# Constant-product filler on TensorE in the idle stretches of a scheduled four-layer bf16 kernel

## The chip, the cores and the metric

The kernel runs on one core of a Trainium2 chip. The metric is the device time of one execution in microseconds (us). A run is called fast or slow by whether it lies within 1.5% of the fastest of its kernel. Two kernels count as "faster" or "slower" only beyond 2%. Engines are named as in the profile: PE is TensorE's matmuls, PEld its weight loads, ACT is ScalarE, DVE is VectorE, POOL is GpSimd, SP is SyncE.

## The reference

Four residual layers over x of 2048 x 512, in bf16: A, B, A, B, each on the layer-normed x, both A layers with the same weights and both B layers too.

```python
# A: attention with a recurrent memory: 64 segments of 32 tokens, 8 memory rows, 32 heads of 128
for s in range(n_seg):
    h = concat([mem, x[segment s]])            # 40 rows
    q, k, v = h @ Wq, h @ Wk, h @ Wv           # each 512 -> 32 x 128
    p = softmax(where(mask, q k^T * scale, -1e9))
    o = (p v) @ Wo
    mem = o[:, :8];  outs.append(o[:, 8:])     # the memory rows feed the next segment
# B: linear attention, 32 heads of 16
qkv = x @ wqkv
pq, pk = phi(q), phi(k)                        # phi(t) = where(t > 0, t + 1, exp(t)) + 1e-6
o = (pq (pk^T v)) / (pq sum(pk) + 1e-6);  return o @ wo

x = x + A(layernorm(x));  x = x + B(layernorm(x))
x = x + A(layernorm(x));  x = x + B(layernorm(x))
```

The weights Wq, Wk, Wv and Wo have 4 MB each and stay on chip for both A layers. The segments form a chain through `mem`; the last rows of an A layer must be done before the B layer's sum over all tokens is, and so each change of layer is a short serial chain.

## The kernel before

The program is first recorded as nodes (engine, cost, what is read and written), then a list scheduler lays the nodes out on a modelled clock, and that fixes each engine's queue. The chip runs each queue in its order; a node's position is decided by the model's times and by hand-tuned priorities (`OFFSET`), never at run time.

```python
MODE_SLACK = 12.41
LOOK = 0.074

def c_pe4(n_mm, n):                      # model: n_mm products on four column strips, us
    return n_mm / 4.0 * max(0.0255, (n / 2.4 + 3.0) * 1e-3)

    def schedule(self):
        ...
        for nd in nodes:
            nd.prio = nd.tail
            if nd.key is not None and OFFSET:
                step, name, k = nd.key
                nd.prio = -(step * PERIOD + OFFSET[name][k])
        ...
            # in pick_for(e): do not start low-priority PE work if better work is due within LOOK us
            if pick is not None and e == "pe" and any(
                    t <= tn + LOOK and nd.done is None and nd.prio > pick.prio + 1.0 for t, _, nd in pend[e]):
                heapq.heappush(ready[e], (-pick.prio, pick.idx, pick))
                return None
            return pick
```

The loads: Wq, Wk and Wv on ACT's queue, Wo in four parts and then the B weights wqkv (1.5 MB) on SP's queue. The same SP queue also issues the DMA transposes of `turned`.

```python
    P.at(-8000, "ld1")
    add("sp", lambda s: s.dma_start(x_sb[:, 0, :], x_view[0]), 0.4, writes=[("x", 0)], dsem="dx0", lat=2.0)
    ...
        late.append(add("act", lambda a, W=W, v=v: a.dma_start(W[:, :, :], v), 0.5, writes=[nm], dsem="d" + nm, lat=t))
    ...
    for i in range(4):
        ...
        add("sp", lambda s, hs=hs: s.dma_start(Wo_sb[:, hs, :], wo_view[:, hs, :]), 0.9, writes=[("Wo", i)],
                 dsem="dWo%d" % i, after=[late[1 + i // 2]], lat=(12.5, 14.5, 7.3, 9.8)[i])
    add("sp", lambda s: s.dma_start(wqkv_sb[:, :, :], B_wqkv.rearrange("(c p) f -> p c f", p=128)), 0.5,
        writes=["wqkv"], dsem="dwqkv", after=[P.nodes[-1]], lat=5.0)
```

Most products run in a mode of four column strips of 32: one group is four matmuls and four weight loads, eight PE instructions.

```python
        def project(W, key, blk, bkeys, b, urgent):
            ...
                        r = pe.matmul(tl.f32()[32 * j:32 * j + 32, 0:512], blk[:, c, :], W[:, c, o:o + 512],
                                      start=(c == 0), stop=(c == 3), tile_position=(0, 32 * j))
        ...
        for s in range(NSEG):            # the loop over segments of an A layer
            ...
        w = out_block(NSEG)              # last output product, residual, then the B layer's input rows
        residual(NT - 1, 3, w)
        b_in(base + NSEG + 2, NT - 1, not first)
```

The softmax here doesn't subtract the row's maximum and nothing guards it: scores larger than these inputs give would overflow.

## Time and profile before

| kernel before | value |
|---|---|
| time, median of 3 runs | 1845.87 us (1845.44 to 1850.28) |
| span of the profiled run | 1843.1 us |
| PE busy, matmuls / weight loads | 1758.4 us (95%), 46693 / 46693 |
| packets of the instruction queue | 365, 5.98 MB |
| first Wk / Wv / Wo product starts | 25.61 / 39.55 / 51.11 us |
| last residual of layer 1, first Wq product of layer 3 | 900.11, 918.99 us |
| last residual of the second A layer | 1806.27 us |

Here "layer 1" and "layer 3" are the two A layers. PE is the bound except in three places: the first 70 us, where weights load; the 19 us between the layers; and the last 37 us. A page slice is a fortieth of the span; the digits are tenths.

### The profile page before, as it was taken

The page shows a single profiled execution, that of the slowest core. Times are in us where ns is not written, and L with a number is a line of the kernel's source. Part 1 is how long each engine was busy: PE and PEld are TensorE (multiplying, and loading weights), DVE is VectorE, ACT ScalarE, POOL GpSimd, SP SyncE. Part 2 cuts the span into 40 slices and gives each one's busy share as a digit, 9 for nine tenths or more (in the row PEclk, how much of TensorE's full clock was granted, in tenths as well). Part 3 has the DMA queues.
Part 4 walks back from the last instruction along what each step waited for, and adds up shares of the span by engine and source line. Part 5 has one row for each costly group of instructions (what it writes and reads, how often), then busy time and mean ns, then how long its engine had stood idle before and what let it go on. Part 6 is the DMA issues. An engine that isn't in the chain of part 4 may idle for free.

```text
span 1843.1 us, 100858 instructions
## 1 busy us (share of the span) xinstructions
PE 1758.4 (95%) x46693; PEld 1194.1 (65%) x46693; DVE 1017.6 (55%) x3168; ACT 1207.6 (66%) x3127; POOL 76.9 (4%) x182
## 2 busy tenths in 40 slices
PE   5899999999999999999799999999999999999997
PEld 2566676666666767666566666666666666666663
DVE  2355555555555555555545555566555556555566
ACT  3566666766666666666466667666667666666665
POOL 3000000000000000000000000000000000000000
PEclk8999999999999999999899999999999999999999
DMA  9312122212221221211012122122122222122223
GB/s 366 85 37 42 38 44 35 47 38 44 38 41 41 35 46 38 44 37 38 22 29 39 37 41 46 39 42 43 38 41 46 41 43 41 41 43 41 52 62 99
DMA packets 218934, 94.85 MB, mean 51 GB/s; under 512 B 202536, under 2 KB 212656, under 8 KB 216976
## 3 DMA queue, kind: packets, MB, share of 16 engines
q1 hardware_dynamic: 211312, 60.22, 17.7%
q0 software_dynamic: 5616, 15.60, 2.9%
q10 hardware_dynamic: 1584, 12.58, 1.7%
q8 instruction: 365, 5.98, 1.3%
q14 instruction: 57, 0.47, 0.1%
HBM read 29.63 MB, written 10.49 MB: 22 GB/s over the span
## 4 chain that ended last, share of the span: by engine, by line
PE 83%; DMA 11%; ACT 3%; DVE 2%; issue 1%; ACTq 0%; DVEq 0%
PE pb L777 38%; PE pb L987 16%; DMA arena_sb<-arena_sb 9%; PE pb L959 3%; PE pb L861 3%; PE pb L1029 3%; PE pb L799 3%; PE pb L1137 3%; PE pb L916 2%; ACT arena_sb L608 2%; PE pb L878 2%; PE pb L1173 1%; DMA Wk_sb<-in_A_Wk_dram 1%; PE pb L892 1%; PE pb L891 1%
## 5 line engine op out<-in xcount | busy, mean ns | idle before, releaser
L608 ACT ACTIVATE arena_sb<-pb 128x512 bf16<-128x512 f32 (+6 forms) x1412 | 727.2, 523 | 359.8 <-PE pb L777 302.1
L777 PE MATMUL pb<-Wq_sb,arena_sb 128*32 128x512 bf16 x5120 | 357.5, 383 | 0.6 <-DMA Wq_sb<-in_A_Wq_dram 0.6
L777 PE MATMUL pb<-Wv_sb,arena_sb 128*32 128x512 bf16 x5120 | 356.9, 382 | 0.1
L777 PE MATMUL pb<-Wk_sb,arena_sb 128*32 128x512 bf16 x5120 | 343.5, 381 | 6.6 <-DMA Wk_sb<-in_A_Wk_dram 5.2
L987 PE MATMUL pb<-Wo_sb,arena_sb 128*32 128x256 bf16 x10368 | 326.4, 273 | 5.8 <-issue 3.7
L987 PEld LDWEIGHTS pb<-Wo_sb,arena_sb 128*32 128x32 bf16 x10368 | 261.5, 96 | 34.8 <-DVE arena_sb L895 13.8
L944 DVE TENSOR_TENSOR arena_sb<-arena_sb 32x256 bf16<-32x256 bf16 x512 | 213.3, 417 | 119.8 <-ACT arena_sb L940 108.7
L609 DVE CAST arena_sb<-pb 128x128 bf16<-128x128 f32 (+3 forms) x334 | 118.5, 355 | 252.5 <-PE pb L1012 201.4
L609 DVE COPY arena_sb<-pb 128x512 bf16<-128x512 bf16 (+2 forms) x352 | 137.7, 392 | 204.5 <-PE pb L799 198.9
L777 PEld LDWEIGHTS pb<-Wk_sb,arena_sb 128*32 128x32 bf16 x5120 | 141.8, 97 | 126.1 <-DMA Wk_sb<-in_A_Wk_dram 5.3
L777 PEld LDWEIGHTS pb<-Wq_sb,arena_sb 128*32 128x32 bf16 x5120 | 133.4, 97 | 113.6 <-DVE arena_sb L609 24.2
L777 PEld LDWEIGHTS pb<-Wv_sb,arena_sb 128*32 128x32 bf16 x5120 | 134.4, 98 | 86.3 <-issue 4.4
L608 ACT ACTIVATE outW_sb<-pb 128x128 fp32r<-128x128 f32 x261 | 72.3, 277 | 114.4 <-PE pb L987 77.1
L799 PEld LDWEIGHTS pb<-id_sb,arena_sb 128*32 128x32 bf16 x4352 | 77.5, 97 | 90.8 <-ACT arena_sb L608 58.1
L959 PE MATMUL pb<-arena_sb 128*128 128x128 bf16 x1024 | 130.9, 217 | 0.0
L799 PE MATMUL pb<-id_sb,arena_sb 128*32 128x128 bf16 x4352 | 109.6, 221 | 14.7 <-ACT arena_sb L608 14.6
L946 DVE TENSOR_TENSOR arena_sb<-arena_sb 32x64 bf16<-32x64 bf16 x512 | 111.1, 217 | 15.8
L960 PE MATMUL pb<-arena_sb 128*128 128x32 bf16 x1024 | 118.3, 177 | 0.0
L868 ACT ACTIVATE arena_sb<-pb 128x256 bf16<-128x256 f32 x252 | 96.1, 383 | 27.3 <-PE pb L861 20.6
L861 PE MATMUL pb<-arena_sb 128*128 128x32 bf16 x2016 | 97.0, 178 | 5.2 <-DMA arena_sb<-arena_sb 4.9
L895 DVE TENSOR_TENSOR arena_sb<-pb,arena_sb 128x128 bf16<-128x128 f32 x252 | 72.2, 286 | 42.0 <-ACT arena_sb L883 27.6
L861 PEld LDWEIGHTS pb<-arena_sb 128*128 128x128 bf16 x2016 | 74.6, 96 | 30.0 <-DMA arena_sb<-arena_sb 6.4
(121 smaller groups left out, 2304.5 us busy)
## 6 DMA issues: line engine op xcount, KB each, us to landing
arena_sb<-arena_sb SPq DMA_TRANSPOSE x368, 2.5
Wq_sb<-in_A_Wq_dram ACTq DMA_DIRECT2D x1, 4096.0 KB, 13.6
Wk_sb<-in_A_Wk_dram ACTq DMA_DIRECT2D x1, 4096.0 KB, 24.3
Wv_sb<-in_A_Wv_dram ACTq DMA_DIRECT2D x1, 4096.0 KB, 34.6
Wo_sb<-in_A_Wo_dram SPq DMA_DIRECT2D x4, 1024.0 KB, 11.6
xs_scratch<-x_sb POOLq DMA_DIRECT2D x32, 128.0 KB, 2.1
pq_scratch<-arena_sb POOLq DMA_DIRECT2D x32, 128.0 KB, 2.8
x_sb<-xs_scratch POOLq DMA_DIRECT2D x16, 128.0 KB, 2.3
```

Of the source, the lines that this page charges most:

```text
L608: return e.activation(o() if callable(o) else o, i() if callable(i) else i, ACTF.Copy)
L609: return e.tensor_copy(o() if callable(o) else o, i() if callable(i) else i)
L777: r = pe.matmul(tl.f32()[32 * j:32 * j + 32, 0:512], blk[:, c, :], W[:, c, o:o + 512], start=(c == 0), stop=(c == 3), tile_position=(0, 32 ...
L799: r = pe.transpose(tt.bf16()[32 * j:32 * j + 32, 128 * i:128 * i + 128], img[:, k, o:o + 32], id_sb[:, :], tile_position=(0, 32 * j))
L861: r = pe.matmul(tl.f32()[:, o:o + 32], kk[:, hh, :, :].rearrange("p j x -> p (j x)"), qT[:, r2, hh, :, 0:8], start=True, stop=True)
L868: add("act", lambda a: a.activation(Pm[:, k, :, :].rearrange("p a q -> p (a q)"), tl.f32()[:, 0:256], ACTF.Exp, scale=SCALE), c_act(256), ...
L895: add("dve", lambda v: v.tensor_tensor(oTb[:, s % NO, 16 * b:16 * b + 16, 0:8], pv.f32()[:, 0:128].rearrange("p (n q) -> p n q", q=8), Rm[ ...
L944: add("dve", lambda v, q=q, j=j: v.tensor_tensor(Pbx[q, :, j, 0:32], Px[q, :, :], Rx[q, :, :], ALU.mult), c_dve(256) + 0.075, reads=["Px", ...
L946: add("dve", lambda v, q=q, j=j: v.tensor_tensor(Pbx[q, :, j, 32:40], PLL[q, g2, :, gl], Rx[q, :, 0:8], ALU.mult), c_dve(64) + 0.075, read ...
L959: pe.matmul(o, vimg[:, r2, e], Pbx[:, hh, :, 0:32], start=True, stop=False)
L960: return pe.matmul(o[:, :, 0:8], vleft[:, g2, e], Pbx[:, hh, :, 32:40], start=False, stop=True)
L987: r = pe.matmul(tl.f32()[32 * j:32 * j + 32, 0:256], oT[:, 4 * hh + n, :], Wo_sb[:, 8 * n + hh, 256 * d:256 * d + 256], start=(hh == 0 and ...
```

## The change

The intent: PE works at half clock for a while after it idled, so let it run products of two constants (the identity and a tile of ones, into a bank of its own) at the lowest priority wherever it would idle. Then it should be at full clock when the real work comes. All priority offsets were tuned anew with the filler in, and two loads' modelled latency was made more realistic.

```diff
-MODE_SLACK = 12.41
+MODE_SLACK = 12.48
 OFFSET = {
     ... (every offset changed)
+    "warm": (2000.00,),
 }
-    def x_move(o, i, k, reads, writes, kind, eng="pool"):
+    def x_move(o, i, k, reads, writes, kind, eng="pool", lat=2.0):
 ...
-    add("sp", lambda s: s.dma_start(x_sb[:, 0, :], x_view[0]), 0.4, writes=[("x", 0)], dsem="dx0", lat=2.0)
+    add("sp", lambda s: s.dma_start(x_sb[:, 0, :], x_view[0]), 0.4, writes=[("x", 0)], dsem="dx0", lat=8.5)
 ...  (lat=8.5 likewise for the second tile of x in the A layers)
+    def warm(step, n, after):
+
+        P.at(step, "warm")
+        tl = P.tile()
+
+        def mm(pe):
+            for j in range(4):
+                r = pe.matmul(tl.f32()[32 * j:32 * j + 32, 0:128], id_sb[:, 0:32], one_sb[:, :], start=True, stop=True,
+                              tile_position=(0, 32 * j))
+            return r
+        for i in range(n):
+            if i:
+                P.again()
+            add("pe", mm, c_pe4(4, 128), reads=["id", "one"], tiles=[tl], mode="col", after=after if i == 0 else ())
 ...
         prepare(0, -2)
+        if first:
+            warm(base, 210, [n for n in P.nodes if n.key == (base - 2, "prepF", 5)])
 ...
         w = out_block(NSEG)
+        warm(base + NSEG, 230 if first else 170, [P.nodes[-3]])
```

## The prediction

> **What bounds the kernel now.** I read the page first. Its engine table gives TensorE (PE) 95% of a span of 1843.1 us, against 66% for ACT and 55% for DVE, and the chain that ended last is 83% PE. Then I looked for the places where this is not so: the page's 40 slices.
>
> ```profile
> PE   5899999999999999999799999999999999999997
> PEclk8999999999999999999899999999999999999999
> DMA  9312122212221221211012122122122222122223
> ```
>
> PE is full except in the first slice, around slice 20 and at the end, and in the same slices the granted clock (second row) dips. DMA is saturated in the first slice only. Next I asked for the stretches around these places, 5 us each; columns are the window, its length, PE, weight load, DVE, ACT, POOL busy time, granted clock, DMA share, GB/s.
>
> ```profile
> 20.00:25.00 5.00, 0.41 (x16) 0.23 (x16) 0.42 (x1) 0.00 (x1) 2.94 (x9) 0.97 1.01 416
> 25.00:30.00 5.00, 4.38 (x56) 1.97 (x60) 0.30 (x1) 1.19 (x2) 0.00 (x0) 0.50 1.01 418
> ...
> 40.00:45.00 5.00, 5.00 (x51) 1.74 (x44) 2.94 (x10) 1.87 (x5) 0.00 (x0) 0.50 1.03 259
> ...
> 900.00:905.00 5.00, 1.63 (x8) 0.89 (x9) 2.40 (x5) 0.55 (x3) 1.08 (x2) 0.70 0.07 26
> 905.00:910.00 5.00, 4.58 (x32) 2.09 (x30) 2.20 (x7) 1.19 (x2) 0.00 (x0) 0.62 0.10 26
> ```
>
> PE idles, then works at half clock just when it is needed. Cutting windows until the clock was constant gives six cold stretches, each close to 6.83 us long: 24.9 to 31.7, 38.5 to 45.3 and 62.4 to 69.2 while the kernel starts, 902.1 to 908.9 and 915.7 to 922.6 between the layers, 1806.6 to 1813.4 before the last stage. PE is busy in them for 6.07, 6.22, 6.18, 4.61, 4.54 and 3.54 us, 31.2 us together. At half clock up to half of that, **15.6 us or 0.8% of the span, is all that warmth alone can return**. The Wq products at 14.4 us also run cold (629 ns mean, as against 380 in steady state), though the record shows full clock there, as it begins only at 18.0 us; they end long before Wk lands and cost nothing.
>
> **What the Trainium skill says.** "TensorE: Matmul & The Clock Gate", section "Part 1: The HAM clock gate (the "warmup" mystery)", says the array starts at half clock, is released after about a 3.4 us window of activity and throttled again after an idle one, with windows that run free. The trace agrees: the states are 0.50 and 1.00, and cold stretches last two such windows (6.83 us). Under "HAM oscillation — how this bites in real kernels" it asks for no idle gaps above some 3.4 us; here the trace differs: an idle time of 2.5 us (59.9 to 62.4) was followed by a cold stretch, and so was 35.1 to 38.5, where PE was merely half idle. "Part 4: PE-mode transpose" says that transposes don't count as busy for the clock; the filler is a true product, so this favours it. "Runtime: NRT & Kernel Launch", section "Instruction fetch mechanics", says instructions are fetched in blocks of 256 through DMA and that this is mostly hidden. The trace has 365 packets of the instruction queue for 100858 instructions (5.98 MB), so it agrees on the size, but PE shows "issue" waits of 1.2 us at 36.96 and 1.9 us at 1802.5, just when or after DMA is saturated.
>
> **The change part by part.** It adds 210 + 230 + 170 = 610 groups of four products of 128x128 on the four column strips: 2440 matmuls and as many weight loads, 5.2% more than 46693. It takes one group as 56 ns; the transposes of line 799 have the same shape and take 0.22 us for 16 on the chain, so 55 ns for four: agreed, when warm. Added as work this would be 610 x 0.056 = 34 us (1.9%). But the groups have the lowest priority and are placed by the kernel's own scheduler in gaps, and not if better work is due within 0.074 us. PE idles about 12 us before Wv is in, some 10 us between 899.5 and 919 (9.55 of 19.5 us busy) and 4.4 us of the 9.4 from 1805.6 to 1815, so the budgets of 11.8, 12.9 and 9.5 us fit these gaps. I count the filler itself as free, apart from a small delay per real product behind it.
>
> *Start.* Wq lands near 14.3 us, Wk at 25.6, Wv at 1.8 + 34.6 = 36.4; that is bandwidth (416 GB/s at DMA share 1.0), which the filler cannot touch. But Wv's products start at 39.55 only, 3.1 us late:
>
> ```profile
> 25.61 3.60 PE pb L777 x32
> ...
> 36.96 1.23 issue
> ...
> 39.74 5.12 PE pb L777 x47
> ```
>
> This is the chain of waits by time: start, us, what. Warm, the stretch from 25.6 saves some 3.0 us (half of 6.07), so that the backlog is gone when Wv lands; the 48 Wv products (12 rounds of four, 0.43 us each cold, 0.22 warm) save 2.6 us. So 5.7 us of PE time. The next gate is Wo: its last quarters are issued at 38.6 and take 7.8 and about 10 us, landing near 49, and the output product starts at 50.9. That leaves 1.7 us, plus 1.4 to 2.2 us if the issue follows Wv's landing at once (it stands behind a DMA transpose issued at 37.2). I take **3.5 us**, the smaller bound. At 56.0 a DMA transpose takes 6.2 us behind the wqkv load and PE idles 3.05 us, then runs cold; the 210 groups are mostly used by then. If a few are left there, half of 6.18 is saved; I give that one chance in three: **1.0 us**.
>
> *Between the layers.* The chain of waits from 900 to 920:
>
> ```profile
> 903.35 0.62 PE pb L750 x4
> ...
> 904.48 3.61 PE pb L1137 x8
> 908.11 0.61 ACT arena_sb L608
> 908.76 0.41 PE pb L1149 x4
> ...
> 918.01 0.61 PE pb L750 x4
> 918.62 0.43 PE pb L1245 x4
> 919.05 3.75 PE pb L777 x36
> ```
>
> Warm, the eight rows take 1.75 us, but phi(k), which runs beside the second four (1.9 us on ACT and DVE), then ends last, so 1.6 saved; two transposes 0.2 each; lines 1149 and 1245 together 0.2; the 36 products from 919.05 save 1.8. Sum 4.0. Nine PE operations of the chain may find filler in flight or in the wrong place; at one group of 0.056 each plus a change of tiling mode, I take off 0.7 (an estimate from the group's time): **3.3 us**.
>
> *Before the end.* Line 1137 runs four rows on the chain in 1.90 us, warm 0.95; the transpose and the product before it save 0.3; less 0.25 for the filler: **1.0 us**. After that ACT and DVE set the pace, and PE was warm already.
>
> *The new order.* Every priority offset is tuned anew, and the first loads' modelled latency goes from 2.0 to 8.5 us, which is what the profile shows. Steady state has some 2% idle PE, about 35 us over the run; a new order can move that either way. I put 0 +- 5 us.
>
> Sum: 3.5 + 1.0 + 3.3 + 1.0 = 8.8 us, so **1837.0 us**.
>
> **The rivals.** (1) *DMA keeps the start*: the gain of 4.5 shrinks to 1 or 2, because Wo and the wqkv load gate the first steps. DMA share near 1 until 45 us speaks for it; the late Wv products against. Time: 1840. (2) *Filler in the way*: the queue is fixed in order, so filler placed by a model that errs stands before real work, and cold groups take double. The gaps are mostly waits for DMA, though, and the chains' modelled times match (0.60 us for a 512 ACT, 0.70 DVE). If each of the three places loses 2 us: 1843. (3) *Instruction fetch*: 1680 extra instructions while DMA is saturated, about 6.6 blocks; one or two more waits of 1.2 us. For it: the wait at 36.96; against: waits in idle time are free. Time: 1839. (4) *The order decides*: the new offsets cut steady idle by 5 to 8 us: 1830.
>
> **Range and chances.** Start 1.5 to 7, middle 2 to 4.5, end 0.3 to 1.5, order +-5; combined, a gain of 2 to 16 us: 1830 to 1844. For 2% the time must be under 1809 or over 1883; the cold total of 15.6 us and the filler's whole 34 us both stay within that, so "same" is nearly certain.
>
> **What would show it.** Right: no cold stretch left at 25 to 45, at 900 to 922 and at 1807 to 1813, mean clock above 0.995; Wv's products starting at 36.5 and the eight rows near 1.8 us; PE busy share up by about 1%, with no gain from that. The end of the first layer's last output product (899.5 before) shows the start plus the order; from there to about 923 shows the middle. Wrong: filler beside new PE waits, cold stretches at the same places (then constants don't count as activity), "issue" waits that grow, or a shift that grows steadily from 70 to 895 us, which would be the order and not the warmth.

## The result, and the profile after

| | before | after |
|---|---|---|
| median of all 4 runs, us (range) | 1846.95 (1845.44 to 1850.28) | 1873.41 (1871.39 to 1882.19) |
| span of the profiled run | 1843.1 | 1872.7 |
| PE matmuls recorded / weight loads | 46693 / 46693 | 49019 / 49133 |
| packets of the instruction queue | 365 | 384 |
| first Wk / Wv / Wo product | 25.61 / 39.55 / 51.11 | 45.03 / 58.98 / 72.4 |

The kernel takes 1.5% longer: ratio 1.015, 95% interval 1.0114 to 1.0186. That is within 2%, as predicted, but the time lies far above the range of 1830 to 1844, and it is a loss and not a gain. Ratios here are the mean time of one kernel's fast runs over that of the other's of the same rounds, so not quite the ratio of the medians in the table. The weight loads rose by exactly the 2440 of the filler; some matmul records are missing.

By the marks of the two traces the 29.6 us of the spans divide as follows. From the start to the first Wo product: +21.3. From there to the first layer's last residual: 849.0 before, 849.5 after, so +0.5. From that residual to the first Wq product of layer 3: 18.9 before, 24.6 after, +5.7. From there to the second A layer's last residual: 887.3 and 887.4, +0.1. From there to the end: 36.8 and 38.8, +2.0. **The long steady stretches, 94% of the time, did not change by more than one kernel's own scatter (some 4 us a layer, see e9); the loss lies in the three places that were to gain.**

The page's slices of the kernel after, the same three rows as the prediction shows:

```profile
PE   4899999999999999999999999999999999999998
PEclk8899999999999999999999999999999999999999
DMA  8411221221212221212011222222222122222222
```

The dip of PE and clock in the middle is gone from the page (of two cold stretches of 6.8 us one of 3.4 is left, 928.3 to 931.7), so the filler does count as work for the clock. But the start is no warmer, and DMA, which was at 9 and 3 tenths in the first two slices, is at 8 and 4: the same loads are spread out further. The stretches of 5 us, with the columns of the prediction's table:

```profile
25.00:30.00 5.00, 2.92 (x112) 2.92 (x116) 0.00 (x0) 0.00 (x0) 0.00 (x0) 0.71 1.01 416
...
40.00:45.00 5.00, 3.56 (x140) 3.39 (x144) 0.00 (x0) 0.00 (x0) 0.00 (x0) 0.66 0.07 22
```

From 25 to 30 us ACT and DVE do nothing at all, though Wk is there from 25.7; from 40 to 45 us even DMA is nearly idle (share 0.07, before 1.03). What PE does is in its timeline (start, us, engine, line, operation, out<-in, shape, count, and in brackets the idle time ahead and what ended it):

```profile
27.08 3.60 PE L737 MATMUL pb<-one_sb,id_sb 128*32 128x128 bf16 x128 [4.44 <-issue]
34.38 3.38 PE L737 MATMUL pb<-one_sb,id_sb 128*32 128x128 bf16 x128 [3.70 <-issue]
41.12 3.41 PE L737 MATMUL pb<-one_sb,id_sb 128*32 128x128 bf16 x128 [3.37 <-issue]
...
45.03 1.94 PE L793 MATMUL pb<-Wk_sb,arena_sb 128*32 128x512 bf16 x32
```

Line 737 is the filler. It runs in lots of exactly 128 matmuls, which with their 128 loads are 256 instructions, and before each lot PE waits 3.4 to 4.4 us for nothing that the profile shows. The Trainium skill, "Runtime: NRT & Kernel Launch", section "Instruction fetch mechanics", says that instructions come in blocks of 256 over a DMA queue. The lots agree with that number, and so do the packets of queue q8, if they are PE's alone: 365 for 93386 PE instructions before, 384 for 98266 after (twice the weight loads). (The prediction set them against the 100858 of all engines.) In the DMA records of this trace single packets of that queue lie at 24.6, 31.8 and 38.6 us, each about 1.1 us long, and PE goes on about 1.4 us after each ends. The last two start 4.7 and 4.2 us after the first product of the lot before, as if a block were asked for only then. So PE seems starved of instructions: one block per 7.30 us (27.08 to 34.38) and per 6.74 us (34.38 to 41.12). Only after three such blocks come the Wk products, 19.4 us later than before, though Wk landed as early (24.6 us after its issue, before 24.3).

Later work follows. SP's queue in the trace of after:

```profile
53.18 2.11 SPq L806 DMA_TRANSPOSE arena_sb<-arena_sb  x1
55.34 1.19 SPq L647 DMA_DIRECT2D Wo_sb<-in_A_Wo_dram  x2
```

and of before:

```profile
37.23 1.30 SPq L790 DMA_TRANSPOSE arena_sb<-arena_sb  x1
38.59 1.62 SPq L646 DMA_DIRECT2D Wo_sb<-in_A_Wo_dram  x2
```

The second half of Wo stands behind a transpose whose input comes from PE by way of ACT. That transpose is 16 us late, so the load is 16.8 us late, and DMA stands nearly idle between 40 and 55 us (mean share 0.08, before 0.71).

Between the layers the same shows with DMA nearly idle. The chain of waits of after:

```profile
923.60 1.97 PE pb L737 x128
925.57 2.05 issue
927.63 0.35 PE pb L737 x11
```

Again a lot of 128, warm this time (1.97 us), and a wait of 2.05 us: 256 instructions in 4.03 us (923.60 to 927.63), at a DMA share of 0.11. The packet comes 1.4 us after the lot's first product here. And filler is now the chain itself.

### The profile page after: what moved, and what is told of

Same layout as the page of the kernel before. It is cut to its first block, busy times and chain, and to the rows that moved or that the text cites. A ratio compares the mean times of both kernels' runs of the same rounds, so it can differ in the third digit from the quotient of the medians.

```text
span 1872.7 us, 105613 instructions
## 1 busy us (share of the span) xinstructions
PE 1778.8 (95%) x49019; PEld 1232.5 (66%) x49133; DVE 1019.3 (54%) x3175; ACT 1203.5 (64%) x3120; POOL 76.8 (4%) x182
## 4 chain that ended last, share of the span: by engine, by line
PE 81%; DMA 11%; DVE 4%; issue 3%; ACT 2%; POOL 0%; POOLq 0%; ACTq 0%; DVEq 0%
PE pb L793 37%; PE pb L1003 16%; DMA arena_sb<-arena_sb 10%; PE pb L815 3%; PE pb L1045 3%; PE pb L877 3%; PE pb L975 3%; PE pb L737 2%; DVE arena_sb L610 2%; PE pb L1156 2%; PE pb L894 2%; PE pb L932 2%; ACT arena_sb L609 2%; PE pb L1192 1%; PE pb L1274 1%
## 5 line engine op out<-in xcount | busy, mean ns | idle before, releaser
L609 ACT ACTIVATE arena_sb<-pb 128x512 bf16<-128x512 f32 (+5 forms) x1411 | 722.8, 520 | 358.7 <-PE pb L793 294.0
L793 PE MATMUL pb<-Wq_sb,arena_sb 128*32 128x512 bf16 x5120 | 348.9, 380 | 6.0 <-DVE arena_sb L610 5.0
L1003 PE MATMUL pb<-Wo_sb,arena_sb 128*32 128x256 bf16 x10368 | 321.0, 273 | 4.6 <-issue 2.3
L610 DVE CAST arena_sb<-pb 128x32 bf16<-128x32 f32 (+3 forms) x351 | 127.1, 363 | 258.6 <-PE pb L1028 204.2
L610 DVE COPY arena_sb<-pb 128x512 bf16<-128x512 bf16 (+1 forms) x336 | 134.8, 402 | 228.5 <-PE pb L815 218.7
L815 PE MATMUL pb<-id_sb,arena_sb 128*32 128x128 bf16 x4352 | 108.5, 220 | 17.1 <-ACT arena_sb L609 17.1
L877 PEld LDWEIGHTS pb<-arena_sb 128*128 128x128 bf16 x2016 | 74.6, 96 | 31.6 <-DMA arena_sb<-arena_sb 9.3
L975 PEld LDWEIGHTS pb<-arena_sb 128*128 128x128 bf16 x1024 | 89.8, 96 | 5.7 <-issue 1.2
## 6 DMA issues: line engine op xcount, KB each, us to landing
Wk_sb<-in_A_Wk_dram ACTq DMA_DIRECT2D x1, 4096.0 KB, 24.6
```

The lines of the kernel that those rows point to most:

```text
L609: return e.activation(o() if callable(o) else o, i() if callable(i) else i, ACTF.Copy)
L610: return e.tensor_copy(o() if callable(o) else o, i() if callable(i) else i)
L815: r = pe.transpose(tt.bf16()[32 * j:32 * j + 32, 128 * i:128 * i + 128], img[:, k, o:o + 32], id_sb[:, :], tile_position=(0, 32 * j))
L877: r = pe.matmul(tl.f32()[:, o:o + 32], kk[:, hh, :, :].rearrange("p j x -> p (j x)"), qT[:, r2, hh, :, 0:8], start=True, stop=True)
L975: pe.matmul(o, vimg[:, r2, e], Pbx[:, hh, :, 0:32], start=True, stop=False)
L1003: r = pe.matmul(tl.f32()[32 * j:32 * j + 32, 0:256], oT[:, 4 * hh + n, :], Wo_sb[:, 8 * n + hh, 256 * d:256 * d + 256], start=(hh == 0 and ...
```

## The experiments

There are eighteen, each compared with runs of the kernel before on the same chip. "New order" below means the offsets and latencies of the changed kernel.

### e1 to e4: what of the change costs the time

**e1: the new order without filler.**

```diff
-        if first:
-            warm(base, 210, ...)
-        warm(base + NSEG, 230 if first else 170, [P.nodes[-3]])
```

> The new order and the new latency of the first loads, with both calls of the filler taken out. Theory F (instruction supply: the filler's 8 instructions per 56 ns outrun the fetch, and real products stand behind it in PE's queue): the order costs nothing, since layer 2 took 885.2 us after as against 886.6 before; 1840 to 1852 us, and Wk's products start near 25.6 us. Rival O (the new order costs the time): stays above 1862. Rival T (the filler's PE time stands in the way): also near 1846, so this run separates O from F and T only.

Measured: median 1845.91, ratio 1.0002 (0.9979 to 1.0025). Wk, Wv and Wo start at 25.73, 38.41 and 49.64. The new order and latencies cost nothing and gain nothing in the sum; by its trace the first A layer is 3.4 us longer and the second 5.3 us shorter than before.

**e2: the same queue, the same filler time on PE, a quarter of its instructions.** One full-width product takes the place of four strips; the scheduler is told nothing, so all places stay.

```diff
-            for j in range(4):
-                r = pe.matmul(tl.f32()[32 * j:32 * j + 32, 0:128], id_sb[:, 0:32], one_sb[:, :], ..., tile_position=(0, 32 * j))
-            return r
+            return pe.matmul(tl.f32()[:, 0:128], id_sb[:, :], one_sb[:, :], start=True, stop=True)
```

> Each filler group is one full 128x128x128 product in place of four 32-column ones: by the scheduler's costs the same order, place and 56 ns of PE time, but 2 instructions in place of 8 (1220 in place of 4880). Theory F: at 36 instructions per us it stays under the 64 per us that the trace of the changed kernel shows between the layers (one block of 256 per 4.0 us), so the issue waits in the filler go from 22 us to under 4 and the time to 1835 to 1846. Rival T (PE time of filler in the way): nothing changes, 1868 to 1878.

Measured: 1850.52, ratio 1.0032 (1.0012 to 1.0051). PE's timeline:

```profile
21.32 6.76 PE L736 MATMUL pb<-one_sb,id_sb 128*128 128x128 bf16 x118
28.01 1.91 PE L790 MATMUL pb<-Wk_sb,arena_sb 128*32 128x512 bf16 x32
```

118 groups run in 6.76 us without a gap, 57 ns each, and Wk's products start at 28.01, not at 45.03. The page shows a clock of 9 in all slices, though cold stretches remain (38.3 to 41.7, 65.6 to 69.0 and 1809.8 to 1816.7 us, at 0.50). Some 23 of the 28 us are gone with the instructions, in each of the three places: from the start to Wo 51.7 us (after 72.4, before 51.1), between the layers 17.1 (24.6, 18.9), at the end 34.7 (38.8, 36.8). The time still missed the expected 1835 to 1846, because the two A layers took 855.6 and 892.7 us (before 849.0 and 887.3); e14 to e18 look for the cause.

**e3: the same instructions, almost no work.** The filler has 8 columns, not 128.

```diff
-                r = pe.matmul(tl.f32()[32 * j:32 * j + 32, 0:128], id_sb[:, 0:32], one_sb[:, :], ...)
+                r = pe.matmul(tl.f32()[32 * j:32 * j + 32, 0:8], id_sb[:, 0:32], one_sb[:, 0:8], ...)
```

> All 8 instructions of each group are kept, and the order, but the products have 8 columns in place of 128, so PE's array works far less. Theory F: the same instruction count means the same waits for instructions, 1866 to 1882 us (a little more cold clock), Wk's products again start near 45 us. Rival T: with the array time gone the loss goes too, 1842 to 1852.

Measured: 1874.80, ratio 1.0163 (1.0142 to 1.0184): the whole loss, with a sixteenth of the filler's columns.

```profile
26.08 1.19 PE L737 MATMUL pb<-one_sb,id_sb 128*32 128x8 bf16 x128 [5.03 <-issue]
32.83 1.19 PE L737 MATMUL pb<-one_sb,id_sb 128*32 128x8 bf16 x128 [5.55 <-issue]
```

A lot of 128 now takes 1.19 us (in after 3.4 to 3.6), and the wait grows to 5.0 and 5.6 us, so that the period stays at 6.75 us. **The period belongs to the instructions, not to the work in them.** e2 and e3 together settle the main cause: the supply of instructions to PE.

**e4: the fewest instructions.** One product of 512 columns in the place of four groups, with the right cost and mode given to the scheduler.

```diff
+            return pe.matmul(tl.f32()[:, :], id_sb[:, :], one_sb[:, :].unsqueeze(1).to_broadcast([128, 4, 128]), start=True, stop=True)
-        for i in range(n):
+        for i in range(n // 4):
-            add("pe", mm, c_pe4(4, 128), ..., mode="col", ...)
+            add("pe", mm, c_pe(1, 512), ...)
```

> The same budget of PE time in 152 products of 128x512 (304 instructions in place of 4880). Theory F: no issue wait is left in the filler, no cold stretch before 60 us, between the layers or before the end; 1832 to 1842 us, which is what the blind prediction expected of the change itself. Rival T: coarser pieces of 0.22 us stand in the way even more, 1870 or above.

Measured: 1847.99, ratio 1.0016 (0.9997 to 1.0035), mean clock 0.998, above the expected 1832 to 1842. The loss is gone, yet a clock that is full but for 37.2 to 40.7 and 64.6 to 68.0 us gained nothing either. Two lines of its timeline show where the start's gain went:

```profile
21.38 6.43 PE L736 MATMUL pb<-one_sb,id_sb 128*128 128x512 bf16 x29
...
62.25 0.37 PE L874 MATMUL pb<-arena_sb 128*128 128x32 bf16 x8 [2.35 <-DMA arena_sb<-arena_sb]
```

The filler ends at 27.8, 2 us after Wk has landed (25.7), and Wk's first product starts at 27.74, because the model puts more of it there than fits: real work stands behind it. And at 62 us PE waits for a DMA transpose. The same line in e1:

```profile
62.77 0.37 PE L877 MATMUL pb<-arena_sb 128*128 128x32 bf16 x8 [4.21 <-DMA arena_sb<-arena_sb]
```

With or without filler PE goes on at 62.2 to 62.8: what is gained before is waited for there.

At the end the rows run warm (1.67 us), and still the last stage takes 36.9 us (before 36.8), where the small products of e2, of about the same PE time in all, take 34.7: in e4's chain of waits wide filler products of 0.22 us each stand between the real ones, which may be why. So wide is not free either.

### e5 and e6: which place costs how much

**e5: filler in the start only** (the call with 230 and 170 groups removed).

> The changed kernel with its first filler alone (210 groups while the weights load). By the trace of the changed kernel the start costs 21.8 us (the last output product of layer 1 feeds its residual at 921.9 us as against 900.1), so 1863 to 1871 us, with Wk's products again near 45 us and the second half of Wo issued near 55 us. If the loss belonged to the filler as a whole and not to places, it would be a third of it: near 1855.

Measured: 1864.96, ratio 1.0111 (1.0094 to 1.0128), so +20 us. **e6: filler between the layers only** (the other calls removed).

> The changed kernel with its second filler alone (230 groups between the layers). By the trace the stretch from the residual of layer 1 to the first Wq product of layer 2 is 24.6 us as against 18.9, so +5.7: 1848 to 1854 us. Theory F says that the DMA is idle here, so one block of 256 instructions still takes about 4.0 us and the filler outruns it without any weight load beside it. If saturated DMA were needed for the loss, this run would be at 1842 to 1846.

Measured: 1853.93, ratio 1.0055 (1.0039 to 1.0072), +9 to +10 us, of which the trace shows 2.9 in the stretch between the layers (21.8 against 18.9) and the rest later. No load runs there (DMA share 0.02 from 918.25 to 921.73), so a loss does not need a busy DMA. The two add up to the whole loss within the scatter.

### e7 to e9: does the start gain if the transfer at 56 us is moved

**e7: no filler, and the wqkv load cut in four.** Its quarters go out in steps 1 to 4.

```diff
-    add("sp", lambda s: s.dma_start(wqkv_sb[:, :, :], ...), 0.5, writes=["wqkv"], dsem="dwqkv", ..., lat=5.0)
+            if first and 1 <= s <= 4:
+                add("sp", lambda e, c=s - 1: e.dma_start(wqkv_sb[:, c, :], B_wqkv[128 * c:128 * c + 128, :]), 0.5, ..., lat=3.0)
```

> No filler; the load of the 1.5 MB wqkv, which stands ahead of the DMA transposes of step 1 in the same queue, is cut in four and issued after steps 0 to 3. Theory D (in the start the transposes behind that load are the gate: PE idled 4.2 us until 62.8 in the run without filler, and all variants resume at 62.2 to 63): the idle time shrinks to under 1.5 us, 1839 to 1844. Rival: each quarter delays a later transpose by as much, and the time stays at 1846.

Measured: 1840.31, ratio 0.9979 (0.9963 to 0.9995). The first residual product comes at 68.17 and not at 71.08 as in e1 (69.52 in e6, whose start is the same). **e8: the same with e4's wide filler.**

> The wide filler (one 128x512 product for four groups) with the same cut load. Theory D says that the wide filler gained nothing at the start because the transposes came at 62 us whatever PE did before; with the gate gone it should be 2 to 5 us under the kernel without filler and the same cut. Rival P (wide filler is itself placed ahead of Wv's products, which started at 41.9 us as against 38.4 without it): no gain, or 1 to 3 us slower than the kernel without filler.

Measured: 1847.3, ratio 1.0014 (0.9999 to 1.0029). Its first residual product comes at 68.58: no gain over e7, although PE's clock is full from 28 to 61.7 us (then 0.50 until 68.5). The filler again lost what it gave. The whole is 7 us slower than e7, more than either expectation allowed; both A layers are longer (852.1 and 888.7 us, in e7 848.3 and 882.7).

**e9: e7 once more, to see its scatter.**

> The same kernel as e7, once more beside the next three, as the level to compare them with: 1838 to 1844 us.

Measured: 1842.13, ratio 0.997 (0.9934 to 1.0005). A third time, as e16 below, it gave 1844.24. The means of 1840.8, 1842.3 and 1843.9 are one kernel's, so **a difference under some 3 us between two kernels of one run each says nothing here.**

### e10 to e15: filler that costs few instructions, place by place

All of these have e9 as their base (new order, wqkv in four), and the filler as one full product per group.

**e11: filler in the middle (198 groups) and at the end (128).**

> e7 with the quarter-instruction filler (one 128x128x128 product per group) between the layers and before the end only, its number cut to 198 and 128 so that none is left over for the steady state. From the segments of e2: 1.8 us saved between the layers (17.1 as against 18.9) and 2.1 at the end (34.7 as against 36.8): 1835 to 1839 us. If instruction places (theory A) matter more than the gain: 1840 to 1846.

Measured: 1846.25, ratio 0.9996 (0.9966 to 1.0026), a miss of the expected 1835 to 1839. The two places did gain (17.2 and 35.2 us, in e9 18.4 and 37.0), but the second A layer took 892.3 us (884.7).

**e12: a start filler trimmed to 132 groups, as wide products.**

> e7 with the wide filler at the start only, cut to the 33 products that stand ahead of Wk's first product (none behind it). Theory P (in e8 filler stood ahead of Wv's products and made them start at 40.3 us): here Wk starts near 25.8 us and runs warm, Wv's products start at 36.5 to 38.5, and layer 1 ends 1 to 3 us earlier: 1836 to 1841 us. If the start is bound by the loads and transposes anyway, the time equals e7's.

Measured: 1844.13, ratio 0.9984 (0.9953 to 1.0015). Wv's products start at 37.91 (e9: 39.02) and the first residual product at 67.2 (e9: 68.83). Eight traces with the same start and no filler there have 68.17 to 68.89, so the start can gain 1.0 to 1.7 us, if little filler stands before Wk (26.28); in the time of the whole it can't be seen.

**e13: filler before the end only (128).**

```diff
+        if not first:
+            warm(base + NSEG, 128, [P.nodes[-3]])
```

> e7 with the cheap filler before the end only (128 groups of one product). By the segments of e11 the end takes 35.1 us as against 37.0 and nothing before it can change: 1.5 to 2.5 us under e16, about 1839 to 1841. If it isn't under e16, the gain at the end is scatter.

Measured: 1840.95, ratio 0.997 (0.9953 to 0.9986), the best kernel with that of e7. The line of the first rows of its last stage in the chain of waits (start, us, what):

```profile
1808.85 1.67 PE pb L1157 x7
```

and in e16, which has no filler:

```profile
1811.68 3.04 PE pb L1158 x7
```

Of the eight products seven are recorded in each; they take 1.67 us warm and 3.04 cold. The stage takes 35.2 us against 36.7 (e16), 37.0 (e9) and 36.8 (before). The mean times of e13 and e16, from the same rounds, differ by 4.1 us; what the end does not explain of that is not explained.

**e14: filler between the layers only (198).** The edit is e13's with `if first` and 198.

> e7 with the cheap filler between the layers only (198 groups of one product). Segment theory: 1.5 us under e16. Theory L (a filler there makes layer 2 slower, as e11's trace has it): 2 to 6 us over e16.

Measured: 1847.35, ratio 1.0015 (0.9998 to 1.0031). **e15: the same queue with 8 columns in each filler product**, so that it keeps no clock.

```diff
-            return pe.matmul(tl.f32()[:, 0:128], id_sb[:, :], one_sb[:, :], start=True, stop=True)
+            return pe.matmul(tl.f32()[:, 0:8], id_sb[:, :], one_sb[:, 0:8], start=True, stop=True)
```

> e14 with 8 columns per filler product: same instructions, order and PSUM banks, no warmth. Theory L by places or banks: as far over e16 as e14 plus the lost 1.5 us. If e14's loss came with the warm clock itself: equal to e16 within 1.5 us. If e14 has no loss: 0 to 2 us over e16.

Measured: 1850.87, ratio 1.0029 (1.001 to 1.0049). The first Wq products of layer 3 in the chain of waits, e14:

```profile
916.40 2.06 PE pb L787 x36
```

and e15:

```profile
919.83 3.96 PE pb L787 x36
```

The same 36 products at half clock take 3.96 us, and warm 2.06. From the last residual to the end of these products it is 19.2 us in e14, 23.3 in e15 and 22.7 before. The mean times differ by 3.2 us (1850.8 and 1847.6), with runs of e15 that scatter over 9 us. So warmth between the layers is worth some 3 to 4 us, close to the 3.3 predicted. But e14 as a whole is not faster than its base: the second A layer takes 890.6 us in it and 890.9 in e15 (from the first Wq product to the last residual), and 884.7 and 887.1 in e9 and e16. No filler product is left over in that layer, and the real products stand in e9's order. So something that comes with the filler and not with warmth seems to take back the 3 us or more (e7, the same kernel as e9 and e16, has 882.7: its own scatter is 4.4 us).

**e10: 104 more PE instructions (52 small products) at the very start, no filler.** Before e11 to e15 the suspicion was that a shift of every later instruction against the blocks of 256 matters.

> e7 with 52 tiny products (104 instructions) put into one early PE step, where PE idles; order, banks and filler as in e7, only every later PE instruction lies 104 places further on in the 256-instruction blocks, as it does in e8 in layer 1. Theory A (the steady state depends on where the fetches of instruction blocks fall): over 3 us away from e7, toward e8's 1847. If the time stays within 2 us of e7, block positions do not explain why e8 was 7 us slower.

Measured: 1844.31, ratio 0.9985 (0.9952 to 1.0019): no effect to be seen.

### e16 to e18: what slows the layer after the filler

**e16: the base again, as a level on the same chip.**

> The kernel without filler and with the cut wqkv load once more, as the level for e13 to e15: 1838 to 1844 us, and again 3 to 6 us under the kernel before.

Measured: 1844.24, ratio 0.9992 (0.9976 to 1.0007). **e17: the base with its PSUM banks renamed**, as a filler tile renames them.

```diff
-    P = _Prog(nc, banks)
+    P = _Prog(nc, [banks[i] for i in (7, 2, 1, 5, 4, 0, 6, 3)])
```

> e16 with the eight PSUM banks renamed everywhere as e14's filler renames them in layer 2; not one instruction more. If the banks' numbers are what costs e14 and e15 their 7 us in layer 2: 5 to 14 us over e16 (both layers have it), 1847 to 1858. If not: 1839 to 1846.

Measured: 1844.45, ratio 0.9995 (0.9978 to 1.0012): the banks are not it. **e18: 140 more instructions at the start**, the same shift modulo 256 as e14 has in the second A layer.

> e16 with 70 tiny products (140 instructions) in an early PE step: all later PE instructions stand in the fetched blocks where e14's stand in layer 2 (396 more, 140 modulo 256). If the places are what costs: 5 to 14 us over e16. If not: 1839 to 1846, and the cause of layer 2's loss stays open.

Measured: 1847.57 (1841.68 to 1852.47), ratio 1.001 (0.9988 to 1.0031), with 890.6 us for the second A layer in the profiled run, as in e14. But the runs scatter over 11 us, so this neither shows nor excludes the shift. Its trace shows something else, too: the start has no "issue" wait near 37 us (1.2 to 1.7 us in the other traces without filler there), no cold stretch from 31.8 us to the end of the layer, and the first residual product at 64.82, over 3 us earlier than in the eight traces named at e12. So where the blocks end may be worth more at the start than filler is; it is one trace, and no run repeats it.

| kernel | median, us | ratio to before (95%) | second A layer in its trace, us |
|---|---|---|---|
| after | 1873.41 | 1.015 (1.0114 to 1.0186) | 887.4 |
| e3, same instructions, no work | 1874.80 | 1.0163 (1.0142 to 1.0184) | 885.8 |
| e2, quarter of the instructions | 1850.52 | 1.0032 (1.0012 to 1.0051) | 892.7 |
| e4, wide filler | 1847.99 | 1.0016 (0.9997 to 1.0035) | 889.1 |
| e1, no filler | 1845.91 | 1.0002 (0.9979 to 1.0025) | 882.0 |
| e14, middle | 1847.35 | 1.0015 (0.9998 to 1.0031) | 890.6 |
| e16, none, wqkv in four | 1844.24 | 0.9992 (0.9976 to 1.0007) | 887.1 |
| e13, end, wqkv in four | 1840.95 | 0.997 (0.9953 to 0.9986) | 886.8 |

## Why the prediction was wrong

**"I count the filler itself as free": this step failed.** Its cost was looked up as PE time (0.056 us per group; a warm lot of after has 32 groups in 1.97 us, 62 ns each) and as gaps in PE's schedule. It was not set against the supply of instructions. A group is eight instructions in 0.056 us, 143 per us; PE got 256 per 6.7 to 7.3 us (35 to 38 per us) while the loads ran, and 256 per 4.03 us (64 per us) at the middle. By the records 640 filler products stand ahead of Wk's first product in the in-order queue, 532 of them, 133 groups, behind the first Wq product: 1064 instructions, 4.2 blocks. The scheduler took these for 7.5 us. They stretch from 19.53 to 45.03 us, 25.5 us; part of that fell where PE had idled before too, and Wk's products came 19.4 us late. The budgets did not fit the gaps either: 12.9 us of filler for 10 us of idle time and 9.5 for 4.4 by the prediction's own count, and 11.8 at the start for 9.6 and not 12 (PE is busy for 18.2 of the 27.8 us from 11.7 to Wv's first product); in after 33 groups of the middle stand in the second A layer, the last at 1012.9 us.

**The rival "Instruction fetch" was the right mechanism, mis-sized.** It reckoned 6.6 blocks, rightly, and then "one or two more waits of 1.2 us", and put 1839. PE's issue waits just ahead of the filler add up to this, in the trace of after (line, reason, total us, times, longest):

```profile
PE pb L737 <- issue: 22.3, 13, 4.4
```

The mistake was in "waits in idle time are free". With an in-order queue the filler waits, and so does the work behind it, however idle PE was meant to be. The number was to be had beforehand: in the trace of before, PE has "issue" waits of 1.81 us that end at 1797.69 and of 1.91 us that end at 1804.45, and between those ends exactly 128 matmuls and 128 loads run (columns as in the prediction's table):

```profile
1797.69:1804.45 6.76, 4.82 (x128) 4.06 (x128) 0.96 (x3) 1.71 (x5) 0.00 (x0) 1.00 0.89 283
```

That is a block per 6.76 us at a DMA share of 0.89. Six and a half blocks of that are 44 us, for a budget of 11.8.

**Start, predicted gain 3.5 and 1.0, measured loss 21.3.** The loss is the supply (e5: +20 us alone; e2 with a quarter of the instructions: Wo at 51.69, before 51.11). Of the expected gain little was there even so. In e2 and e4 the filler stands in the way of Wk (28.0 and 27.7, against 25.7), as rival "Filler in the way" said, and the transposes at 62 us gate e1 and e4 alike, as "DMA keeps the start" said. The step that took Wo as the last gate failed: trimmed filler left Wo's first product where it was (49.86 us, after a wait of 1.38 for its DMA; in e9 49.90) and gained 1.0 to 1.7 us by the first residual product, with the wqkv load cut up (e12).

**Between the layers, predicted gain 3.3, measured loss 5.7.** The worth of warmth was right: 3 to 4 us between e14 and e15. The allowance of 0.7 for filler in the way was too small, for the same cause: in after the eight rows start, by their first weight load, 7.5 us after the last residual (929.42 and 921.9), before 4.4 us (904.48 and 900.11). In e2, the same queue with a quarter of the instructions, the stretch takes 17.1 us and so gains 1.8.

**End, predicted gain 1.0, measured loss 2.0.** Warmth is worth more than predicted, 1.5 to 1.9 us (e13 against e16 and e9); in after the filler's instructions took it and more (e2: 34.7 us, after 38.8).

**The new order, 0 +- 5: right, in part by luck.** e1 has 1.0002, but as a sum of +3.4 and -5.3 us in the two A layers. "Same" within 2% also held, but not by the argument given: the loss was bounded by the filler's 34 us of PE time, and supply has no such bound (its 19 blocks at 6.7 us each would be 128 us, an estimate).

**What would show it.** Full clock came before the end, as predicted (at 1834 to 1841 in after), and between the layers (922 to 947 in after) but for 928.3 to 931.7, where most of the eight rows ran. At the start the cold stretches moved but stayed (27.1, 34.0 and 40.8 us and later ones), since starved filler keeps no clock. Of the signs named for "wrong", '"issue" waits that grow' is the one that came true.

**What stays open.** In seven kernels with filler between the layers the second A layer takes 888.7 to 892.7 us, and in nine of the new order without it 882.0 to 887.1. But after and e3 (887.4 and 885.8, with filler) don't fit that, nor does e18 (890.6, without). In e8 and e7 PE's real work in that layer stands in the same order. Warmth is not the cause (e15), nor the banks (e17). A shift against the instruction blocks remains possible, and isn't shown (e10, e18).

## What to carry to other kernels

Price an added instruction by the fetch as well as by the engine: count instructions per us that the queue asks for, and compare with the rate at which blocks were seen to come in the same stretch; a kernel's own trace gives it, where a busy engine shows "issue" waits one block apart. Filler must be few instructions, but not long ones (e4's wide products gained nothing at the end, e13's did), and must end before the real work's data lands, since an in-order queue turns its delays into those of everything behind it, even of loads issued by another engine. The best version here, e13, keeps the filler only where no load runs and the chain after it is PE's, and cuts the large load that held up small transposes; its gain of 0.3% (ratio 0.997) is far within the 2% that count as the same.

## What the Trainium skill lacked or had wrong

- "Runtime: NRT & Kernel Launch", "Instruction fetch mechanics", calls the cost of a block boundary mostly hidden and says fetch is hidden by the slower dispatch. Here PE executes 256 short instructions in 1.19 us (e3) and gets them once per 6.75 us while loads run (6.76 us in the kernel before, at a DMA share of 0.89), and per 4.03 us (after) and 3.48 us (e6: lots start at 918.25 and 921.73) with DMA nearly idle. No rate is given on the page; these runs show 35 to 41 PE instructions per us beside the loads (e5, 256 in 6.19 us from 27.08 to 33.27, is the quickest) and 64 to 74 where DMA was nearly idle. The steady state here needs 51 per us (93386 in 1843.1 us). In after, e3 and e6 a block's packet starts 4.0 to 4.7 us after the first product of the lot before beside the loads, and 1.2 to 1.4 us after it with DMA nearly idle; PE goes on 1.3 to 1.6 us after the packet's end. The page gives none of these times.
- "TensorE: Matmul & The Clock Gate", "HAM oscillation — how this bites in real kernels", speaks of idle gaps above 3.4 us. Waits of 3.4 to 4.4 us between lots of filler let the clock fall, as it says: it was 0.71 and 0.66 in the stretches 25 to 30 and 40 to 45 us. In the kernel before less was enough: it fell at 62.3 us, 2.4 us after PE had stopped, and at 38.4 us, where PE had been busy for 2.06 of the last 3.41 us and no gap was longer than 1.23 us.
- "DMA: Bandwidth & Descriptors", "Issuing engines are not separate DMA queues", says that transfers of different engines interleave. It gives no figure for what a small one pays that was issued behind a large one from the same engine: the transpose behind the 1.5 MB load took 6.2 us (the median is 2.5), and cutting that load in four brought the first residual product forward, to 68.17 to 68.89 us in eight traces, from 71.08 in e1 and 69.52 in e6.
